# Wider rows for q and causal k, paired P1 blocks, earlier first outputs and later transposes in an attention-plus-MLP kernel

## Chip, cores and metric

One core of a Trainium2 chip. The metric is the device time of one execution in microseconds (us). Times are medians of several executions, with the range in brackets. The profile is one execution of the same program; its span is some 1.8 us shorter than the time of the same execution.

A ratio of two kernels is the mean time of one kernel's runs over that of the other's of the same rounds, so it is not quite the ratio of the medians that are quoted. Its 95% interval stands in brackets behind it.

## The reference

Four batches of eight heads, 768 tokens, head dimension 64. Three heads attend causally ("retrieval"); five see only four sink tokens and a window of 64. The attention output goes through a two-layer MLP with a per-feature leaky slope.

```python
# q, k, v: (4, 8, 768, 64) float32; is_retrieval = [1,0,1,0,0,0,1,0]; n_sink 4, window 64
scores = matmul(q, k.T) / sqrt(64)
mask   = causal                      # retrieval heads
mask   = causal & (sink | in_window) # the other heads
a = softmax(where(mask, scores, -1e9)); attn = matmul(a, v)
x = attn.transpose(0, 2, 1, 3).reshape(3072, 512)
h = x @ w_in                                   # (512, 2048)
out = (max(h, 0) + alpha * min(h, 0)) @ w_out  # (2048, 512)
```

## The kernel before

Work goes in 16 pairs of heads, four to a batch. "P1" is the product with w_in, "P2" the one with w_out. Pairs 0 to 3 run while data and weights load. Then the first P1 block follows, and from pair 4 on P1 and P2 of the last batch fill TensorE between the attention pieces. All of q, k and v are loaded as float32, cast to bfloat16, and transposed on TensorE for pairs 0 to 7. The parts that matter here:

```python
def load_pair(n, src, dst, eng):              # q or k of both heads: ONE transfer, rows of two tokens (512 B)
    flat = dst.rearrange("p a b d -> p (a b d)")[:, 0:12 * D]
    T = rows_of(n)                            # 2 for pairs 0 to 7, 1 after
    eng.dma_start(flat.rearrange("p (x y) -> p x y", y=T * D),
                  dram(src, base, [[T * D, 128], [128 * T * D, 12 // T], [1, T * D]]))

def load_v(n): ...                            # one transfer for each head, and a short one for a windowed head

gate = const.tile([128, 1], fp32, name="gate")
nc.gpsimd.tensor_copy(gate, vf[2][:, 5, 1, D - 1:D])   # weights start only after v of pair 2
load_w_in(0, 512)                                      # GpSimd issues the weights, q4 and v4 follow on SyncE
...
for n in range(4):                            # pairs 0 to 3
    ...
    if n == 3:                                # k of pair 4 is issued by ScalarE, between exponentials of pair 3
        seq.insert(1, lambda: load_k(4, nc.scalar))
...
# pair n, from 4 on: sa, sb are the score pieces of its two heads, nxt the transposes of pair n + 1
seq = sa[:1] + prev + sa[1:3] + tail + sa[3:5] + nxt[:1] + sa[5:] + nxt[1:] + sb[:1]
seq += [lambda: AV(n, 0)] + sb[1:]
```

The softmax here doesn't subtract the row's maximum and nothing guards it: scores larger than these inputs give would overflow.

Of the kernel before, what the change touches and what calls it, by code (L numbers as in the profile page):

```python
# [8 lines left out]
AF = mybir.ActivationFunctionType  # L9
# [5 lines left out]
def kernel(  # L15
# [89 lines left out]
    def heads(n):  # L105
        return PAIRS[n % 4]

    def rows_of(n):
        return 2 if n < CROSS else 1

    def load_pair(n, src, dst, eng):
        flat = dst.rearrange("p a b d -> p (a b d)")[:, 0:12 * D]
        base = (n // 4 * H + heads(n)[0]) * S * D

        T = rows_of(n)
        eng.dma_start(flat.rearrange("p (x y) -> p x y", y=T * D),
                      dram(src, base, [[T * D, 128], [128 * T * D, 12 // T], [1, T * D]]))

    def load_q(n, eng=nc.sync):
        load_pair(n, q, qf[n % NF], eng)  # L120

    def load_k(n, eng=nc.sync):
        if n >= CROSS:
            load_rows(n, k, kf)
        else:
            load_pair(n, k, kf[n % NF], eng)
# [29 lines left out]
    def cast_pair(n, nat, src, *copies):  # L156
        copy = copies[0]
        flat = src.rearrange("p a b d -> p (a b d)")[:, 0:12 * D]
        if n >= CROSS:
            copy(nat.rearrange("p i (h d) -> p h i d", h=2), flat.rearrange("p (h i d) -> p h i d", h=2, d=D))  # L160
            return
        pairs = flat.rearrange("p (h i t d) -> p h i t d", h=2, t=2, d=D)
        for t in range(2):
            copies[t % len(copies)](nat[:, 3 * t:3 * t + 3, :].rearrange("p i (h d) -> p h i d", h=2), pairs[:, :, :, t, :])

    def whole_q(n):
        nat = natq[n] = NAT0[0][n] if n < 4 else NATQ[n % 2]
        copy = nc.gpsimd.tensor_copy if 0 < n < 6 else nc.scalar.copy if 0 < n < CROSS else nc.vector.tensor_copy
        cast_pair(n, nat, qf[n % NF], copy)
        if n >= CROSS:  # L170
            nc.sync.dma_start(qT[n % NK][:, 0:S].rearrange("p (i r) -> p i r", r=128),
                              nat.rearrange("p i c -> p (i c)"), transpose=True)

    def whole_k(n):
        if n < CROSS:
            natk[n] = NAT0[1][n] if n < 4 else NATK1[n % 2]
            one = nc.gpsimd.tensor_copy if 0 < n < 6 else nc.vector.tensor_copy
            cast_pair(n, natk[n], kf[n % NF], one, nc.scalar.copy if n == 0 else one)
            return
# [94 lines left out]
    def Tq(n):  # L274
        tr = T_bank(natq.pop(n), "mm0" if n < 4 else misc_tag())
        T = rows_of(n)
        nc.scalar.copy(qT[n % NK][:, 0:S].rearrange("d (p t) -> d p t", t=T), in_order(tr[:, 0:S], T))

    def Tk(n):
        tr = T_bank(natk.pop(n), "mm1" if n < 4 else misc_tag())  # L280
        T = rows_of(n)
        for hh, h in enumerate(heads(n)):
            rows = slice(64 * hh, 64 * hh + 64)
# [3 lines left out]
            if RETR[h]:  # L287
                cuts = [0, 256 // T, S // T] if n == 0 else [0, S // T]
# [109 lines left out]
    def X(n):  # L398
        nat = xn.pop(n)
        tr = bank_bf(misc_tag())  # L400
        for i in range(NT):
# [9 lines left out]
    BANKS = {"beside P2": ["mm0", "mm1"], "beside attention": ["mm0", "mm1", "mm2", "m2"],  # L411
             "lead": ["mm0", "mm1", "mm2", "m2", "sc0", "sc1"], "tail": ["mm0", "mm1", "sc0", "sc1"]}
# [7 lines left out]
    def P1(t, f, cs=range(4), where="beside P2"):  # L420
        o, w = TOK[t]
        o %= 2 * S
        psg = half_done.pop((t, f)) if (t, f) in half_done else mm_bank(where)
        for c in cs:
            a = PAIRS[c][0] // 2
            nc.tensor.matmul(psg[:, 0:w], w_in_b[:, a, 128 * f:128 * (f + 1)], xT[:, c, o:o + w],  # L426
                             start=(c == 0), stop=(c == 3))
        if cs[-1] < 3:
# [3 lines left out]
        nc.scalar.activation(neg[:, 0:w], psg[:, 0:w], AF.Relu, scale=-1.0)  # L432
        nc.vector.scalar_tensor_tensor(g_buf[t % 2][:, f, 0:w], neg[:, 0:w], oma[:, f:f + 1], psg[:, 0:w],  # L433
                                       op0=ALU.mult, op1=ALU.add)

    po = {}
    n_po = [0]

    def P2(t, s, quarter):
        if quarter == 0:  # L440
            n_po[0] += 1
            tags = ("mm2", "m2", "m0", "m1") if t > 5 else ("mm2", "m2")
            po[t] = bank(tags[n_po[0] % len(tags)])
        for f in range(4 * quarter, 4 * quarter + 4):
            nc.tensor.matmul(po[t], g_buf[t % 2][:, f, 128 * s:128 * (s + 1)], w_out_b[:, f, :],  # L445
                             start=(f == 0), stop=(f == 15))
        if quarter == 3:
            ot = work.tile([128, 512], fp32, tag="ot", name="ot", bufs=3)
            nc.scalar.copy(ot, po.pop(t))  # L449
# [19 lines left out]
    def p1_units(t, fs=range(16), where="beside P2"):  # L469
        return [(TOK[t][1] / 512, lambda f=f: P1(t, f, where=where)) for f in fs]  # L470

    def p2_units(t):
        return [(1, lambda s=s, u=u: P2(t, s, u)) for s in range(TOK[t][1] // 128) for u in range(4)]
# [11 lines left out]
    def seg_pieces(n):  # L485
# [6 lines left out]
        seq += [lambda: AV(n, 0)] + sb[1:]  # L492
        return seq, (2 + len(sa[1:3]) if tail else 0)
# [15 lines left out]
    gate = const.tile([128, 1], fp32, name="gate")  # L509
    nc.gpsimd.tensor_copy(gate, vf[2][:, 5, 1, D - 1:D])  # L510
# [30 lines left out]
    for n in range(4):  # L541
# [5 lines left out]
        else:  # L547
            seq = [sa[0], last[0], sa[1], last[1]] + sb + [last[2]]
# [18 lines left out]
    AV(3, 0)  # L567
# [46 lines left out]
    second = [p2_units(t) for t in range(8)]  # L614
    hidden = [p1_units(t) for t in range(6)]
    hidden[1][:6] = p1_units(1, range(6), where="beside attention")
    plan = [hidden[1][:6] + merge(second[0], hidden[1][6:]) + second[1][:4],
# [58 lines left out]
```

## Time and profile before

| | before |
|---|---|
| median of 4 runs beside the changed kernel | 251.75 us (250.34 to 252.37) |
| profiled span | 249.1 us |
| TensorE busy | 233.9 us, 94% |
| ScalarE busy | 144.7 us, 58% |
| first score matmul, first w_in matmul, pair 4's first score matmul, first w_out matmul | 7.18, 28.01, 42.88, 53.51 us |
| last matmul ends | 245.83 us |

The prediction below shows the lines that find the bound: TensorE is full except in the loading phase and at the end, and its one large hole is a wait of 5.1 us for q of pair 5 that ends at 51.5 us. The columns are start, time, engine, line, operation, count, and in brackets the idle time before it with what ended it; "ACTq" is ScalarE's sequencer. Short names from here on: "q4" is q of pair 4; natq and natm are the bfloat16 copies of q and k; eR and eS are the exponentials of the causal and of the windowed heads; g holds the hidden values of the MLP; Tq(n), Tk(n) and X(n) are the transposes of q, of k and of the attention output of pair n; sa, sb are the score pieces of its two heads, nxt the transposes of pair n + 1.

### The profile page before, as it was taken

The page shows a single profiled execution, that of the slowest core. Times are in us where ns is not written, and L with a number is a line of the kernel's source. Part 1 is how long each engine was busy: PE and PEld are TensorE (multiplying, and loading weights), DVE is VectorE, ACT ScalarE, POOL GpSimd, SP SyncE. Part 2 cuts the span into 40 slices and gives each one's busy share as a digit, 9 for nine tenths or more (in the row PEclk, how much of TensorE's full clock was granted, in tenths as well). Part 3 has the DMA queues.
Part 4 walks back from the last instruction along what each step waited for, and adds up shares of the span by engine and source line. Part 5 has one row for each costly group of instructions (what it writes and reads, how often), then busy time and mean ns, then how long its engine had stood idle before and what let it go on. Part 6 is the DMA issues. An engine that isn't in the chain of part 4 may idle for free.

```text
span 249.1 us, 5404 instructions
## 1 busy us (share of the span) xinstructions
PE 233.9 (94%) x2059; PEld 146.8 (59%) x2059; DVE 166.6 (67%) x399; ACT 144.7 (58%) x289; POOL 49.0 (20%) x104
## 2 busy tenths in 40 slices
PE   7799799479999999999999999999999999999994
PEld 6688545346767655455667645456676544456653
DVE  7788688617698987888678757976556546743320
ACT  5888188527777567666655656566654355543320
POOL 5559820540104210110102110200000000000000
PEclk9999999959999999999999999999999999999999
DMA  6997999999999998999795981311111101012112
GB/s 191 267 241 143 229 202 197 218 251 266 241 235 142 230 236 182 222 175 188 131 230 121 229 132 45 71 37 43 45 42 42 45 0 42 3 42 84 45 45 84
DMA packets 90882, 34.95 MB, mean 140 GB/s; under 512 B 72408, under 2 KB 89064, under 8 KB 90856
## 3 DMA queue, kind: packets, MB, share of 16 engines
q1 hardware_dynamic: 83448, 24.77, 51.3%
q0 software_dynamic: 5664, 8.91, 15.8%
q10 hardware_dynamic: 1744, 0.93, 1.4%
q8 instruction: 16, 0.26, 0.4%
q14 instruction: 10, 0.08, 0.1%
HBM read 27.46 MB, written 6.29 MB: 136 GB/s over the span
## 4 chain that ended last, share of the span: by engine, by line
PE 62%; DMA 13%; SPq 8%; DVE 8%; ACT 3%; POOL 2%; issue 2%; POOLq 0%; DVEq 0%; ACTq 0%
PE P L445 27%; PE P L426 22%; DMA qf<-in_q_dram 10%; SPq L137 4%; DMA kf<-in_k_dram 4%; PE P L389 3%; SPq L139 3%; PE P L335 3%; DVE g L433 3%; PE P L362 2%; PE P L402 2%; ACT neg L432 1%; PE P L463 1%; PE P L267 1%; POOL vb L191 1%
## 5 line engine op out<-in xcount | busy, mean ns | idle before, releaser
L433 DVE SCALAR_TENSOR_TENSOR g<-neg,oma,P 128x512 bf16<-128x512 f32 (+1 forms) x128 | 77.5, 613 | 48.2 <-ACT neg L432 46.4
L426 PE MATMUL P<-xT,w_in_b 128*128 128x512 bf16 (+1 forms) x512 | 101.2, 327 | 1.4 <-DVE g L433 1.3
L445 PE MATMUL P<-w_out_b,g 128*128 128x512 bf16 x368 | 94.8, 382 | 0.0
L432 ACT ACTIVATE neg<-P 128x512 f32<-128x512 f32 (+1 forms) x128 | 62.9, 493 | 53.3 <-PE P L426 50.1
L426 PEld LDWEIGHTS <-w_in_b 128*128 128x128 bf16 x512 | 48.1, 98 | 34.7 <-issue 2.2
L445 PEld LDWEIGHTS <-g 128*128 128x128 bf16 x368 | 34.4, 98 | 27.4 <-issue 0.6
L343 ACT ACTIVATE eR<-P 128x455 bf16<-128x455 f32 (+3 forms) x63 | 37.9, 608 | 11.5 <-PE P L335 9.3
L369 ACT ACTIVATE eS<-P 128x384 bf16<-128x384 f32 (+1 forms) x55 | 27.8, 519 | 8.7 <-PE P L362 8.1
L452 POOL DMA_DIRECT2D out_dram<-ot x18 | 9.8, 543 | 94.3 <-ACT ot L449 74.9
L335 PE MATMUL P<-qT,kT 128*128 128x454 bf16 (+10 forms) x132 | 24.6, 271 | 1.0 <-DVE kT L290 0.5
L449 ACT COPY ot<-P 128x512 f32<-128x512 f32 x23 | 13.5, 586 | 13.9 <-PE P L445 13.8
L373 DVE TENSOR_TENSOR eS<-eS,ms 128x384 bf16<-128x384 bf16 (+1 forms) x47 | 16.8, 362 | 6.2 <-ACT eS L369 6.1
L362 PE MATMUL P<-qT,kT 128*128 128x192 bf16 (+2 forms) x140 | 20.1, 236 | 0.8 <-ACT eR L343 0.6
L395 DVE TENSOR_TENSOR xn<-P,rcp 128x448 bf16<-128x448 f32 x32 | 20.0, 625 | 1.1
L362 PEld LDWEIGHTS <-kT 128*128 128x128 bf16 x140 | 13.2, 98 | 7.2 <-issue 0.3
L335 PEld LDWEIGHTS <-kT 128*128 128x128 bf16 x132 | 11.6, 98 | 9.5 <-issue 0.9
L347 DVE TENSOR_TENSOR eR<-eR,mr 128x128 bf16<-128x128 bf16 (+4 forms) x54 | 11.3, 226 | 6.5 <-ACT eR L343 6.4
L389 PEld LDWEIGHTS <-eS 128*128 128x128 bf16 x260 | 10.5, 97 | 3.0 <-DVE eS L373 0.4
L153 POOL COPY natk<-natk 4x192 f32<-4x192 f32 x10 | 4.3, 442 | 40.3 <-DVE natk L182 40.3
L389 PE MATMUL P<-vb,eS 128*128 128x65 bf16 x260 | 11.8, 193 | 0.5 <-DVE xT L404 0.3
L389 PEld LDWEIGHTS <-eR 128*128 128x128 bf16 x324 | 11.3, 97 | 1.5
L389 PE MATMUL P<-vb,eR 128*128 128x65 bf16 x324 | 11.7, 192 | 0.0
(82 smaller groups left out, 164.6 us busy)
## 6 DMA issues: line engine op xcount, KB each, us to landing
qf<-in_q_dram SPq DMA_DIRECT2D x16, 384.0 KB
vf<-in_v_dram SPq DMA_DIRECT2D x32, 192.0 KB
out_dram<-ot POOLq DMA_DIRECT2D x18, 256.0 KB, 2.9
kf<-in_k_dram SPq DMA_DIRECT2D x16, 192.0 KB
kf<-in_k_dram SPq DMA_DIRECT2D x6, 384.0 KB
w_in_b<-in_moe_w_in_dram POOLq DMA_DIRECT2D x4, 512.0 KB, 8.5
w_out_b<-in_moe_w_out_dram POOLq DMA_DIRECT2D x4, 512.0 KB, 18.5
out_dram<-ot SPq DMA_DIRECT2D x5, 256.0 KB
```

The source lines that it names most:

```text
L335: nc.tensor.matmul(sc[:, x, a - lo:z - lo], kt[:, 128 * j:128 * (j + 1)], qt[:, c:c + z - a], start=True, stop=not masked)
L343: nc.scalar.activation(e[:, lo:hi].rearrange("p (x c) -> p x c", x=len(parts)), sc[:, 0:len(parts), 0:(hi - lo) // len(parts)], AF.Exp, sc ...
L362: nc.tensor.matmul(sc[:, x, o:o + w], kt[:, 128 * j:128 * (j + 1)], qt[:, 124 * j:124 * j + w], start=True, stop=not on_pe)
L369: nc.scalar.activation(slots, sc[:, 0:len(thirds), 0:384].rearrange("p x (s c) -> p x s c", c=192), AF.Exp, scale=scale)
L373: nc.vector.tensor_tensor(slots, slots, factor, op=ALU.mult)
L389: nc.tensor.matmul(pav[:, i, :], e[:, o:o + 128], vv[:, j, hh, 0:D + 1], start=(m == 0), stop=(m == len(terms) - 1))
L395: nc.vector.tensor_tensor(xn[n][:, :, 64 * hh:64 * hh + 64], pav[:, :, 0:D], rcp.to_broadcast([128, NT, D]), op=ALU.mult)
L426: nc.tensor.matmul(psg[:, 0:w], w_in_b[:, a, 128 * f:128 * (f + 1)], xT[:, c, o:o + w], start=(c == 0), stop=(c == 3))
L432: nc.scalar.activation(neg[:, 0:w], psg[:, 0:w], AF.Relu, scale=-1.0)
L433: nc.vector.scalar_tensor_tensor(g_buf[t % 2][:, f, 0:w], neg[:, 0:w], oma[:, f:f + 1], psg[:, 0:w], op0=ALU.mult, op1=ALU.add)
L445: nc.tensor.matmul(po[t], g_buf[t % 2][:, f, 128 * s:128 * (s + 1)], w_out_b[:, f, :], start=(f == 0), stop=(f == 15))
L449: nc.scalar.copy(ot, po.pop(t))
```

## The change

The intent: fewer, larger packets for q and causal k, so that q of pair 5 is in earlier; pair 5's transposes later; first outputs that need only the part of w_out that has come; fewer instructions on ScalarE. The core of the diff (the helpers that only follow from it are cut):

```diff
+    def row_tokens(n, h=None):
+        return 1 if n >= CROSS else 6 if h is None or RETR[h] else 2
     def load_q(n, eng=nc.sync):
-        load_pair(n, q, qf[n % NF], eng)
+        T = row_tokens(n)                     # 6: rows of 1536 B
+        eng.dma_start(..., dram(q, ..., [[T * D, 128], [128 * T * D, 12 // T], [1, T * D]]))
     def load_k(n, eng=nc.sync):
-            load_pair(n, k, kf[n % NF], eng)
+        for hh, h in enumerate(heads(n)):     # one transfer for each head
+            T = row_tokens(n, h)
+            eng.dma_start(..., dram(k, ..., [[T * D, 128], [128 * T * D, 6 // T], [1, T * D]]))
 ...
     def P1(t, f, ...):
+        blocks = range(f, f + 512 // w)       # two blocks where the tile has 256 tokens
+        for i, fb in enumerate(blocks): ...
-        nc.scalar.activation(neg[:, 0:w], psg[:, 0:w], AF.Relu, scale=-1.0)
+        nc.scalar.activation(neg, psg, AF.Relu, scale=-1.0)
 ...
+        if n == 4:
+            seq = sa + sb[:1] + [lambda: AV(n, 0)] + sb[1:] + nxt
 ...
-    gate = const.tile([128, 1], fp32, name="gate")
-    nc.gpsimd.tensor_copy(gate, vf[2][:, 5, 1, D - 1:D])
     load_w_in(0, 512)
 ...
-            seq = [sa[0], last[0], sa[1], last[1]] + sb + [last[2]]
+            seq = [sa[0], last[0], sa[1], last[1]] + sb + [lambda: AV(3, 0), last[2]]
 ...
+    second[0] = p2_units(0, [(s + i, u) for s in (0, 2) for u in range(4) for i in range(2)])
-    plan = [hidden[1][:6] + merge(second[0], hidden[1][6:]) + second[1][:4],
+    plan = [merge(second[0], hidden[1]) + second[1][:4],
```

More of the change, by code (lines that the diff above doesn't have):

```diff
@@ L106, in heads @@
         return PAIRS[n % 4]
-    def rows_of(n):
-        return 2 if n < CROSS else 1
-    def load_pair(n, src, dst, eng):
-        flat = dst.rearrange("p a b d -> p (a b d)")[:, 0:12 * D]
-        base = (n // 4 * H + heads(n)[0]) * S * D
-        T = rows_of(n)
-        eng.dma_start(flat.rearrange("p (x y) -> p x y", y=T * D),
-                      dram(src, base, [[T * D, 128], [128 * T * D, 12 // T], [1, T * D]]))
+    def row_tokens(n, h=None):
+        return 1 if n >= CROSS else 6 if h is None or RETR[h] else 2
     def load_q(n, eng=nc.sync):
-        load_pair(n, q, qf[n % NF], eng)
+        T = row_tokens(n)
+        for_heads = qf[n % NF].rearrange("p a b d -> p (a b d)")[:, 0:12 * D]
+        eng.dma_start(for_heads.rearrange("p (x y) -> p x y", y=T * D),
+                      dram(q, (n // 4 * H + heads(n)[0]) * S * D, [[T * D, 128], [128 * T * D, 12 // T], [1, T * D]]))
     def load_k(n, eng=nc.sync):
@@ L124, in load_k @@
             load_rows(n, k, kf)
-        else:
-            load_pair(n, k, kf[n % NF], eng)
+            return
+        for hh, h in enumerate(heads(n)):
+            T = row_tokens(n, h)
+            dst = kf[n % NF].rearrange("p a b d -> p (a b d)")[:, 6 * D * hh:6 * D * (hh + 1)]
+            eng.dma_start(dst.rearrange("p (x y) -> p x y", y=T * D),
+                          dram(k, (n // 4 * H + h) * S * D, [[T * D, 128], [128 * T * D, 6 // T], [1, T * D]]))
     def load_v(n):
@@ L153, in sinks @@
                 nc.gpsimd.tensor_copy(vh[:, 1:7, :], vh[:, 0:1, :].to_broadcast([NSINK, 6, D // 2]))
-    def cast_pair(n, nat, src, *copies):
-        copy = copies[0]
-        flat = src.rearrange("p a b d -> p (a b d)")[:, 0:12 * D]
-        if n >= CROSS:
-            copy(nat.rearrange("p i (h d) -> p h i d", h=2), flat.rearrange("p (h i d) -> p h i d", h=2, d=D))
-            return
-        pairs = flat.rearrange("p (h i t d) -> p h i t d", h=2, t=2, d=D)
-        for t in range(2):
-            copies[t % len(copies)](nat[:, 3 * t:3 * t + 3, :].rearrange("p i (h d) -> p h i d", h=2), pairs[:, :, :, t, :])
     def whole_q(n):
@@ L168, in whole_q @@
         copy = nc.gpsimd.tensor_copy if 0 < n < 6 else nc.scalar.copy if 0 < n < CROSS else nc.vector.tensor_copy
-        cast_pair(n, nat, qf[n % NF], copy)
+        flat = qf[n % NF].rearrange("p a b d -> p (a b d)")[:, 0:12 * D]
+        copy(nat.rearrange("p i (h d) -> p h i d", h=2), flat.rearrange("p (h i d) -> p h i d", h=2, d=D))
         if n >= CROSS:
@@ L176, in whole_k @@
             natk[n] = NAT0[1][n] if n < 4 else NATK1[n % 2]
-            one = nc.gpsimd.tensor_copy if 0 < n < 6 else nc.vector.tensor_copy
-            cast_pair(n, natk[n], kf[n % NF], one, nc.scalar.copy if n == 0 else one)
+            for hh, h in enumerate(heads(n)):
+                copy = nc.gpsimd.tensor_copy if 0 < n < 6 else nc.scalar.copy if n == hh == 0 else nc.vector.tensor_copy
+                T = row_tokens(n, h)
+                flat = kf[n % NF].rearrange("p a b d -> p (a b d)")[:, 6 * D * hh:6 * D * (hh + 1)]
+                copy(natk[n][:, :, D * hh:D * (hh + 1)].rearrange("p (t i) d -> p t i d", t=T),
+                     flat.rearrange("p (i t d) -> p t i d", t=T, d=D))
             return
@@ L275, in Tq @@
         tr = T_bank(natq.pop(n), "mm0" if n < 4 else misc_tag())
-        T = rows_of(n)
+        T = row_tokens(n)
         nc.scalar.copy(qT[n % NK][:, 0:S].rearrange("d (p t) -> d p t", t=T), in_order(tr[:, 0:S], T))
@@ L280, in Tk @@
         tr = T_bank(natk.pop(n), "mm1" if n < 4 else misc_tag())
-        T = rows_of(n)
         for hh, h in enumerate(heads(n)):
+            T = row_tokens(n, h)
             rows = slice(64 * hh, 64 * hh + 64)
@@ L287, in Tk @@
             if RETR[h]:
-                cuts = [0, 256 // T, S // T] if n == 0 else [0, S // T]
+                cuts = [0, -(-256 // T), S // T] if n == 0 else [0, S // T]
                 for lo, hi in zip(cuts, cuts[1:]):
@@ L408 @@
     n_mm = [0]
-    BANKS = {"beside P2": ["mm0", "mm1"], "beside attention": ["mm0", "mm1", "mm2", "m2"],
-             "lead": ["mm0", "mm1", "mm2", "m2", "sc0", "sc1"], "tail": ["mm0", "mm1", "sc0", "sc1"]}
+    BANKS = {"beside P2": ["mm0", "mm1"], "lead": ["mm0", "mm1", "mm2", "m2", "sc0", "sc1"], "tail": ["mm0", "mm1", "sc0", "sc1"]}
     def mm_bank(where):
@@ L423, in P1 @@
         psg = half_done.pop((t, f)) if (t, f) in half_done else mm_bank(where)
-        for c in cs:
-            a = PAIRS[c][0] // 2
-            nc.tensor.matmul(psg[:, 0:w], w_in_b[:, a, 128 * f:128 * (f + 1)], xT[:, c, o:o + w],
-                             start=(c == 0), stop=(c == 3))
+        blocks = range(f, f + 512 // w)
+        for i, fb in enumerate(blocks):
+            for c in cs:
+                a = PAIRS[c][0] // 2
+                nc.tensor.matmul(psg[:, w * i:w * (i + 1)], w_in_b[:, a, 128 * fb:128 * (fb + 1)], xT[:, c, o:o + w],
+                                 start=(c == 0), stop=(c == 3))
         if cs[-1] < 3:
@@ L431, in P1 @@
         neg = work.tile([128, 512], fp32, tag="neg", name="neg", bufs=3)
-        nc.scalar.activation(neg[:, 0:w], psg[:, 0:w], AF.Relu, scale=-1.0)
-        nc.vector.scalar_tensor_tensor(g_buf[t % 2][:, f, 0:w], neg[:, 0:w], oma[:, f:f + 1], psg[:, 0:w],
-                                       op0=ALU.mult, op1=ALU.add)
+        nc.scalar.activation(neg, psg, AF.Relu, scale=-1.0)
+        for i, fb in enumerate(blocks):
+            c = slice(w * i, w * (i + 1))
+            nc.vector.scalar_tensor_tensor(g_buf[t % 2][:, fb, 0:w], neg[:, c], oma[:, fb:fb + 1], psg[:, c],
+                                           op0=ALU.mult, op1=ALU.add)
     po = {}
@@ L442, in P2 @@
             tags = ("mm2", "m2", "m0", "m1") if t > 5 else ("mm2", "m2")
-            po[t] = bank(tags[n_po[0] % len(tags)])
+            po[t, s] = bank(tags[n_po[0] % len(tags)])
         for f in range(4 * quarter, 4 * quarter + 4):
-            nc.tensor.matmul(po[t], g_buf[t % 2][:, f, 128 * s:128 * (s + 1)], w_out_b[:, f, :],
+            nc.tensor.matmul(po[t, s], g_buf[t % 2][:, f, 128 * s:128 * (s + 1)], w_out_b[:, f, :],
                              start=(f == 0), stop=(f == 15))
@@ L448, in P2 @@
             ot = work.tile([128, 512], fp32, tag="ot", name="ot", bufs=3)
-            nc.scalar.copy(ot, po.pop(t))
+            nc.scalar.copy(ot, po.pop((t, s)))
             r = TOK[t][0] + s * 128
@@ L467, in P2_last, with p1_units, p2_units @@
             (nc.scalar, nc.sync)[half].dma_start(out[r:r + 128, c], ot[:, 0:256])
-    def p1_units(t, fs=range(16), where="beside P2"):
-        return [(TOK[t][1] / 512, lambda f=f: P1(t, f, where=where)) for f in fs]
-    def p2_units(t):
-        return [(1, lambda s=s, u=u: P2(t, s, u)) for s in range(TOK[t][1] // 128) for u in range(4)]
+    def p1_units(t, where="beside P2"):
+        return [(1, lambda f=f: P1(t, f, where=where)) for f in range(0, 16, 512 // TOK[t][1])]
+    def p2_units(t, order=None):
+        order = order or [(s, u) for s in range(TOK[t][1] // 128) for u in range(4)]
+        return [(1, lambda s=s, u=u: P2(t, s, u)) for s, u in order]
     def seg_scores(n):
@@ L566 @@
         load(n)
-    AV(3, 0)
     AV(3, 1)
@@ L614 @@
     second = [p2_units(t) for t in range(8)]
+    second[0] = p2_units(0, [(s + i, u) for s in (0, 2) for u in range(4) for i in range(2)])
     hidden = [p1_units(t) for t in range(6)]
-    hidden[1][:6] = p1_units(1, range(6), where="beside attention")
-    plan = [hidden[1][:6] + merge(second[0], hidden[1][6:]) + second[1][:4],
+    plan = [merge(second[0], hidden[1]) + second[1][:4],
             merge(second[1][4:], hidden[2]) + merge(second[2], hidden[3]) + second[3][:2],
```

## The prediction

> **What bounds the kernel now.** I read the page's slices, then the waits, then the order of time on TensorE, SyncE, ScalarE and the DMA queues between 20 and 65 us. The slices first; one is 6.2 us:
>
> ```profile
> PE   7799799479999999999999999999999999999994
> PEclk9999999959999999999999999999999999999999
> DMA  6997999999999998999795981311111101012112
> ```
>
> TensorE is full except at the start, in slice 8 (from 43.6 us) and at the end; slice 9 runs at half clock. The DMA engines are full from 6 us to about 100 us. So TensorE bounds the time, and its one large hole lies in the loading phase. The waits name it:
>
> ```profile
> POOL natq L164 <- DMA qf<-in_q_dram: 7.2, 2, 5.4
> PE P L267 <- POOL natq L164: 5.1, 1, 5.1
> ```
>
> and TensorE's timeline shows it:
>
> ```profile
> 45.80 0.60 PE L426 MATMUL P<-xT,w_in_b 128*128 128x256 bf16 x4
> 51.53 0.95 PE L267 MATMUL P<-ident,natq 128*128 128x128 bf16 x6 [5.12 <-POOL natq L164]
> 52.27 1.06 PE L426 MATMUL P<-xT,w_in_b 128*128 128x256 bf16 x4
> ```
>
> TensorE stands 5.1 us because the transposes of q of pair 5 sit in the middle of pair 4 and that q lands at 50.9. The same four 256-column matmuls then run at half clock; the windows agree (PEclk is the number before the DMA share):
>
> ```profile
> 45.00:50.00 5.00, 1.40 (x12) 0.84 (x10) 2.75 (x10) 2.27 (x7) 3.53 (x8) 0.94 1.21 219
> 50.00:55.00 5.00, 3.47 (x17) 2.06 (x18) 0.97 (x3) 1.73 (x3) 1.91 (x4) 0.50 1.07 252
> ```
>
> From 51.5 to about 55.5 the work done takes 4 us instead of 2: the hole costs 5.1 + 2.0 = 7.1 us. From 56 us on TensorE issues nearly back to back: 0.86 us for four 512-column matmuls, 0.43 for four of 256.
>
> Why is q so late? SyncE issued it at 34.63. In the DMA view from 35 to 45 us:
>
> ```profile
> q0 software_dynamic: 1555, 1.54, 90.7%
> q1 hardware_dynamic: 1556, 0.43, 30.5%
> ```
>
> q0 carries the weights, q1 q, k and v. They alternate one packet for one packet: 10 us x 16 engines / 1555 = 103 ns for a pair, of which the weight packet has some 84 and the 256-byte packet 19. A queue's progress beside the weights is counted in packets, not bytes. Until 50.9 q1 had to pass q4 (768 packets of 512 B), v4 (about 1584 of 256 B) and q5 (768): 195 per engine.
>
> **What the Trainium skill says.** "DMA: Bandwidth & Descriptors", section "Queues, rings and completion order": each engine goes round its queues at packet granularity. The 1555 against 1556 above agrees. The same page, "Why small descriptors are slow": a fixed cost per packet. Here 512-byte loads alone move about 290 GB/s and 256-byte ones about 215 (rates in slices of the window from 5 to 10 us), thus 28 and 19 ns a packet per engine. The packet records give 47 ns for 1 KB and 87 for 2 KB, so I put a 1536-byte packet at about 70 ns, an estimate between these, against 3 x 28 = 84 for what it replaces. "TensorE: Matmul & The Clock Gate", "The HAM clock gate": about 3.4 us of idleness halves the clock, and about as much work restores it. The trace agrees: after a 5.1 us gap half clock until about 55.5. "PSUM — Partial Sum Buffer", "The four PSUM rules": groups open together in one bank spoil each other. The new P1 finishes its first block before it starts the second, so this costs nothing; no run here shows it.
>
> **The change part by part.**
>
> *Six-token rows.* q of pairs 0 to 7 goes from 48 to 16 packets per engine, a causal k head from 24 to 8. In engine time that is only 16 x (84 - 70) = 0.22 us for a q and 0.11 for a k head. Up to k of pair 3 that saves 3 x 0.22 + 2 x 0.11 = 0.9 us, and the first q perhaps 0.4 us more. So k of pair 3, which GpSimd waited for until 18.78, comes about 1.3 us earlier. Beside the weights the gain is larger, as it is packets that count. The casts of q become one instruction instead of two (on ScalarE 0.93 for the two, about 0.85 for one); nothing on the path.
>
> *The gate removed.* The first w_in load is issued at 20.28 after v of pair 2 (20.09); without the gate it follows the cast of k of pair 3, 0.4 us sooner. Its first packets come about 2.5 us after the issue (the DMA rate is near zero from 21 to 22.7 us), by which time v of pair 3 is in. With the rows, w_in and q4 (released behind it) start 1.3 + 0.4, say 1.8 us earlier.
>
> *Pair 5 at the end of pair 4.* Its transposes move some 8 us of TensorE work later. New landing of q5: q4 16 + v4 99 + q5 16 = 131 rounds instead of 195; 131 x 84 = 11.0, plus own packets 1.1 + 1.9 + 1.1 and k4 1.2, is 16.3 us. The same sum for before gives 22.3, and measured was 25.4 (the slowest engine lags), so x 1.14: 18.6 us from 23.6, about 42 us. k5, 32 rounds on, about 46. Pair 4 starts at 42.2 (0.9 us earlier: 0.4 from the first q, and 0.5 as AV(3,0) fills the 1.0 us idle at 26.4). Its TensorE work is 3.1 us of scores, values and transposes and six units of 0.86, 8.3 us in all. Tq(5) comes at about 50: no wait. The 5.1 us and the half clock are gone.
>
> *First outputs by parts of w_out.* This makes the filling possible. The parts land at 41.3, 44.7, 48.3 and 52.3 us now (last packets of q0), in about the same places afterwards: 1.8 us earlier start against about 1.3 more of q and k passed between. With two token tiles taken part by part, parts 0 and 1 are all that pair 4 needs, part 2 comes at about 52, part 3 at about 56. No wait.
>
> *Two 256-token blocks per bank.* ScalarE loses 32 x (2 x 389 - 597) ns = 5.8 us of its 144.7; VectorE and TensorE keep theirs. After 56 us TensorE waits only 1.3 us in all on P1's banks, mostly for 512-token blocks. Worth 0 to 0.3 us.
>
> *What takes over.* Total DMA work is nearly conserved, so the next load is hardly earlier: q of pair 6. ScalarE casts it ahead of the first exponential of pair 5:
>
> ```profile
> 59.77 0.93 ACT L164 CAST natq<-qf 128x384 bf16<-128x384 f32 x2
> 60.58 1.25 ACT L343 ACTIVATE eR<-P 128x454 bf16<-128x454 f32 x2
> ```
>
> Before, q6 landed at about 56.4 (v5 was cast at 55.29, then 48 packets of 28 ns). After: 1.8 earlier by the start, 0.9 by cheaper packets (q4, q5, q6, half of k4 and k5), so 53.7. The cast then ends at 54.6 and the first exponential at 55.2. TensorE reaches pair 5 at 50.5, gets through two score pieces, a value product and two units by about 51.7, and stands until 55.2, as both score banks are full. The third score piece of pair 5 started at 61.94 before: 61.94 - 55.2 = **6.7 us gained**. Of the 8.5 us otherwise within reach (7.1 and the earlier start) some 2 are lost to this new wait. The loads of pair 8 have about 6 us of slack (landed by about 69.5, v cast at 75.3), so they follow. The rest shifts unchanged: 251.7 - 6.7 = 245.0.
>
> **The rivals.** (1) *The new 3.5 us stand trips the clock too.* It is at the edge of the 3.4 us window; half clock would cost 1.7 to 2 us: gain about 4.8, 246.9 us. I give it a third. (2) *The stall moves whole:* as the DMA bytes are conserved, q6 comes no earlier than before, for instance if the earlier w_in does not materialise. The profile speaks for conservation (DMA full from 25 to 60), against it that DMA stands almost still from 21 to 22.7. The gain is then 61.94 - 57.9 = 4.0, 247.7 us; a fifth. (3) *Nothing takes over:* SyncE, whose issues took up to 9 us for v5, runs ahead with fewer packets and q6 comes by 51; all 8.5 us: 243.2. One tenth. (4) *w_in or w_out late:* larger q4 packets delay w_in's last part (landed 37.9, used at about 38.8). It starts 1.8 earlier, so at most 0.5 us is lost.
>
> **Range and chances.** Mixing 245.0 with rivals 1 to 3 gives about 245.7. The range runs from rival 3 to somewhat beyond rival 2, 243.2 to 248.6. The border of 2% is 246.7; rivals 1 and 2 are beyond it, but not all of their mass, so faster 0.65, same 0.33, slower 0.02.
>
> **What would show it.** Right, if the wait of Tq for natq of 5.1 us is gone; w_in is issued near 18.5; the first P2 matmul lies near 43 instead of 53.5; a wait of ScalarE for q of pair 6 appears at 51 to 55 with a TensorE gap of 2 to 4 us; ScalarE's busy time falls by about 6 us, TensorE's matmuls stay. Wrong, if q5 still lands after 48, if TensorE waits for w_out, or if time is gained or lost after 70 us.

## More of the kernel before

One more view matters afterwards: ScalarE's order of time around the load that it issues itself.

```profile
23.13 0.81 ACT L369 ACTIVATE eS<-P 128x768 bf16<-128x768 f32 x1 [0.26 <-PE P L362]
23.21 0.39 ACTq L116 DMA_DIRECT2D kf<-in_k_dram  x1
24.11 0.49 ACT L369 ACTIVATE eS<-P 128x384 bf16<-128x384 f32 x1 [0.17 <-PE P L362]
```

The issue of k of pair 4 takes the sequencer 0.39 us, beside a running exponential. It costs nothing.

## The result, and the profile after

The changed kernel takes 259.13 us (258.36 to 260.18, 4 runs) against 251.75: ratio 1.030 [1.025, 1.036]. It is slower, and outside the predicted range.

| | before | after |
|---|---|---|
| median | 251.75 us | 259.13 us |
| profiled span | 249.1 | 256.6 |
| TensorE busy, matmuls | 233.9, 2059 | 233.5, 2059 |
| first score matmul | 7.18 | 8.09 |
| first w_in matmul | 28.01 | 39.49 |
| pair 4's first score matmul | 42.88 | 54.55 |
| first w_out matmul | 53.51 | 56.72 |
| last matmul ends | 245.83 | 253.31 |

The slices of the page after (6.4 us each) beside those in the prediction:

```profile
PE   7699039979899999999999999999999899999994
PEclk9999858999999999999999999999999999999999
DMA  7999999999923999999394891131101101011212
```

TensorE has the same work. The hole that was in slice 8 is gone, but slices 5 and 6 (25.7 to 38.5 us) hold a larger one, and it has its own half clock. The windows give its size (span of time, then busy time and count of PE, weight loads, VectorE, ScalarE and GpSimd, then clock, DMA share and GB/s):

```profile
25.00:30.00 5.00, 0.98 (x19) 0.83 (x16) 1.18 (x3) 0.00 (x0) 3.12 (x5) 0.96 1.13 238
30.00:35.00 5.00, 0.00 (x0) 0.00 (x0) 0.00 (x0) 0.00 (x0) 1.27 (x2) 0.50 1.22 197
35.00:40.00 5.00, 3.45 (x41) 3.00 (x41) 2.63 (x8) 1.68 (x3) 0.00 (x0) 0.51 1.20 215
```

From 30 to 35 us TensorE, VectorE and ScalarE all do nothing. The waits say who holds whom (engine, tile, line, what ended the wait, total, times, longest):

```profile
ACT eS L365 <- DMA vf<-in_v_dram: 11.0, 1, 11.0
...
PE P L358 <- ACT eS L365: 10.6, 2, 10.4
```

TensorE waits for an exponential on ScalarE (the score banks are full), and ScalarE waits for a load of **v**. No exponential reads v. So look at what ScalarE's sequencer does there:

```profile
24.04 0.81 ACT L365 ACTIVATE eS<-P 128x768 bf16<-128x768 f32 x1 [0.26 <-PE P L358]
24.06 11.64 ACTq L125 DMA_DIRECT2D kf<-in_k_dram  x2
35.80 1.19 ACT L365 ACTIVATE eS<-P 128x384 bf16<-128x384 f32 x2 [10.95 <-DMA vf<-in_v_dram]
```

The same place that took 0.39 us before now holds two issues and takes 11.64. The chain of work shows what lies between the two (start, time, what):

```profile
23.38 11.84 DMA vf<-in_v_dram
...
35.24 0.04 ACTq L125
...
35.31 0.39 ACTq L125
...
35.80 0.50 ACT eS L365
...
36.34 0.32 PE P L358
```

ScalarE's second issue starts only after v of pair 4, issued by SyncE at 23.38, has landed. The program as compiled names the wait. (A semaphore is a counter on which one instruction waits until another has raised it.) Each ordinary transfer of SyncE and ScalarE is given one of eight completion semaphores, DMAHW0 to DMAHW7, in turn; a transfer carries a wait for the previous transfer with the same semaphore. (In the lists of before and after, this holds for each of their 134 and 142 transfers but the first eight.) Building the kernels gives the list of instructions with their waits; the traces do not name semaphores. Shortened, on ScalarE before and after, and the transfer of v on SyncE after (a wait can stand on a semaphore instruction just ahead of the transfer):

```
before  ACT  DMACopy kf <- in_k  128x6x128   [waits DMAHW4, DVE]
after   ACT  DMACopy kf <- in_k  128x384     [waits DMAHW1]
after   ACT  DMACopy kf <- in_k  128x3x128   [waits DMAHW3, DMAHW2, DVE]
after   SP   DMACopy vf <- in_v  128x6x64    [waits DMAHW3]      (v of pair 4, first head)
```

Reckoned in the order of allocation, the turn goes q4 on semaphore 2, v4 on 3, 4 and 5, q5 on 6, k5 on 7 and 0, k4's first half on 1, one transfer of v5 on 2, k4's second half on 3. That is the semaphore of v4's first head, and v4 travels beside the weights: 11.84 us. The single k4 of before had semaphore 4, last used by v of pair 3, which had landed by then.

One thing the prediction did foretell is there as well: with the q rows there is no wait for natq any more. Two new waits of TensorE come with the rest of the change:

```profile
PE P L445 <- DVE g L433: 1.8, 1, 1.8
...
PE P L331 <- ACT kT L286: 0.9, 1, 0.9
```

The sums agree roughly: pair 4 starts 11.7 us later (54.55 against 42.88), the end is 7.5 us later (253.31 against 245.83). Of the difference, 4.2 us, the vanished hole gave back 7.1 and the two new waits took 2.7: 4.4. (By windows of the kernel before, 56.00 to 56.20 us is still at 0.50 and 56.20 to 56.50 at 0.98. So the half clock lasted to 56.2 and not to 55.5, the hole cost nearer 5.1 + 4.7 / 2 = 7.5 us, and the sum is 4.8.)

### The profile page after: what moved, and what is told of

Its sections match the earlier page's. It is cut to its first block, busy times and chain, and to the rows that moved or that the text cites. A ratio compares the mean times of both kernels' runs of the same rounds, so it can differ in the third digit from the quotient of the medians.

```text
span 256.6 us, 5348 instructions
## 1 busy us (share of the span) xinstructions
PE 233.5 (91%) x2059; PEld 147.2 (57%) x2059; DVE 163.9 (64%) x398; ACT 142.8 (56%) x255; POOL 47.9 (19%) x98
## 4 chain that ended last, share of the span: by engine, by line
PE 77%; DMA 8%; DVE 5%; ACT 5%; issue 1%; POOL 1%; ACTq 0%; SPq 0%; DVEq 0%; POOLq 0%
PE P L445 30%; PE P L424 29%; DMA vf<-in_v_dram 7%; PE P L385 6%; PE P L331 4%; PE P L358 3%; DVE g L433 3%; PE P L398 2%; ACT neg L430 2%; DMA qf<-in_q_dram 2%; PE P L463 1%; ACT eR L339 1%; PE P L263 1%; DVE xn L391 1%; POOL vb L187 1%
## 5 line engine op out<-in xcount | busy, mean ns | idle before, releaser
L433 DVE SCALAR_TENSOR_TENSOR g<-neg,oma,P 128x512 bf16<-128x512 f32 (+1 forms) x128 | 74.8, 612 | 49.3 <-ACT neg L430 47.7
L424 PE MATMUL P<-xT,w_in_b 128*128 128x512 bf16 (+1 forms) x512 | 95.7, 326 | 1.4 <-DVE g L433 1.4
L445 PE MATMUL P<-w_out_b,g 128*128 128x512 bf16 x368 | 92.1, 379 | 1.8 <-DVE g L433 1.8
L430 ACT ACTIVATE neg<-P 128x512 f32<-128x512 f32 x96 | 57.1, 598 | 60.3 <-PE P L424 55.2
L339 ACT ACTIVATE eR<-P 128x455 bf16<-128x455 f32 (+3 forms) x63 | 37.6, 604 | 13.6 <-PE P L331 10.6
L365 ACT ACTIVATE eS<-P 128x384 bf16<-128x384 f32 (+1 forms) x55 | 27.8, 519 | 21.5 <-DMA vf<-in_v_dram 11.0
L385 PEld LDWEIGHTS <-eS 128*128 128x128 bf16 x260 | 11.3, 100 | 4.1 <-DVE eS L369 0.8
L385 PE MATMUL P<-vb,eS 128*128 128x65 bf16 x260 | 12.5, 198 | 0.9 <-DVE eS L369 0.6
L153 POOL COPY vb<-vb 4x192 f32<-4x192 f32 x20 | 7.0, 363 | 26.1 <-DVE vb L187 24.9
```

Of the source, the lines that this page charges most:

```text
L339: nc.scalar.activation(e[:, lo:hi].rearrange("p (x c) -> p x c", x=len(parts)), sc[:, 0:len(parts), 0:(hi - lo) // len(parts)], AF.Exp, sc ...
L365: nc.scalar.activation(slots, sc[:, 0:len(thirds), 0:384].rearrange("p x (s c) -> p x s c", c=192), AF.Exp, scale=scale)
L385: nc.tensor.matmul(pav[:, i, :], e[:, o:o + 128], vv[:, j, hh, 0:D + 1], start=(m == 0), stop=(m == len(terms) - 1))
L424: nc.tensor.matmul(psg[:, w * i:w * (i + 1)], w_in_b[:, a, 128 * fb:128 * (fb + 1)], xT[:, c, o:o + w], start=(c == 0), stop=(c == 3))
L430: nc.scalar.activation(neg, psg, AF.Relu, scale=-1.0)
L433: nc.vector.scalar_tensor_tensor(g_buf[t % 2][:, fb, 0:w], neg[:, c], oma[:, fb:fb + 1], psg[:, c], op0=ALU.mult, op1=ALU.add)
```

## The experiments

Theory A: the wait of ScalarE's second k transfer for its completion semaphore stops ScalarE and, through full score banks, TensorE. Rival B: the other parts are to blame (order of P1 and P2, pair 5 late, no gate). Rival C: the second transfer waits for its queue or for room beside the weights. Fifteen kernels ran, all with correct results; e1 to e8 ran on one chip, e9 to e15 on another. Runs of the kernel before went beside each batch, and those of earlier batches on the same chip are counted in: medians of 251.23 us for e1 to e4, 251.72 for e5 to e8, 251.14 for e9 to e12, 251.16 for e13 to e15.

### Is it the split of k? (e1, e2, e3)

**e1**: the changed kernel, k of pair 4 alone in one transfer.

```diff
+        if n == 4:    # one transfer for both heads, two-token rows; Tk and whole_k take T = 2 for it
+            eng.dma_start(kf..., dram(k, ..., [[2 * D, 128], [256 * D, 6], [1, 2 * D]])); return
```

> The changed kernel with k of pair 4 alone loaded by one transfer (two-token rows) instead of two. Theory A (the second of the two transfers on ScalarE's queue reuses the completion semaphore of v of pair 4, which is still in flight, and holds up the exponentials behind it from 24 to 35 us): the 11 us wait of ScalarE and the 10.4 us gap of TensorE at 26 us vanish, pair 4 starts near 43.5 us instead of 54.6, time about 248.5 us, 246 to 251. Theory B (the wider rows and the earlier weights slow the loads themselves, and the order on ScalarE does not matter): still above 256 us with a gap of 8 us or more before 40 us.

Measured: 247.15 us (247.09 to 248.34), ratio 0.983 [0.977, 0.989]; 12 us less than the changed kernel. ScalarE's order of time:

```profile
23.97 0.81 ACT L369 ACTIVATE eS<-P 128x768 bf16<-128x768 f32 x1 [0.26 <-PE P L362]
24.07 0.42 ACTq L123 DMA_DIRECT2D kf<-in_k_dram  x1
24.95 0.49 ACT L369 ACTIVATE eS<-P 128x384 bf16<-128x384 f32 x1 [0.17 <-PE P L362]
```

The stand is gone, and with it the whole loss. B is out for the loss. The bytes are the same.

**e2**: the changed kernel, both transfers of k4 issued by SyncE.

```diff
-            seq.insert(1, lambda: load_k(4, nc.scalar))
+            seq.insert(1, lambda: load_k(4))
```

> The changed kernel with both transfers of k of pair 4 issued by SyncE instead of ScalarE. Theory A: no wait of ScalarE near 24 us, as nothing stands before its exponentials; but k of pair 4 now lies behind v of pair 4, lands near 40 to 43 us and may hold Tk(4) up by 0 to 2 us: about 249.5 us, 247 to 252. Theory B: above 256 us as before.

Measured: 250.68 us (249.67 to 253.14), ratio 0.997 [0.989, 1.005]. ScalarE goes through its exponentials, but k4 comes late. GpSimd waits 11.0 us for it in one piece, of which TensorE passes on 0.7:

```profile
POOL natm L173 <- DMA kf<-in_k_dram: 14.5, 3, 11.0
...
PE P L263 <- POOL natm L173: 0.7, 1, 0.7
```

Off the engine that has the exponentials, the split costs far less. Why e2 is still 3.5 us above e1 is not settled: in the profiled execution 2.2 us of it were there before the weights were used at all (first w_in matmul 30.59 against 28.40; the clock was at half from 8.4 to 11.8 us), and that is not the late k4.

**e3**: the kernel before with nothing but each k load split into two transfers.

```diff
-            load_pair(n, k, kf[n % NF], eng)
+            for hh in range(2):   # one head each, two-token rows as before
+                eng.dma_start(..., dram(k, ..., [[2 * D, 128], [256 * D, 3], [1, 2 * D]]))
```

> The kernel before with nothing changed but that k of each pair up to 7 is loaded by two transfers of one head each, in two-token rows as before. Theory A: the same wait of ScalarE appears, from about 23.5 us until the first head of v of pair 4 lands at 38 to 40 us; part of it is given back as q of pair 5 no longer comes late: 257 to 263 us. Theory B (wide rows or early weights at fault): within 1% of before, 250 to 254 us.

Measured: 261.30 us (258.68 to 261.71), ratio 1.038 [1.031, 1.046]. ScalarE waits for the same load:

```profile
ACT eS L372 <- DMA vf<-in_v_dram: 12.2, 1, 12.2
```

The split alone, without a single changed row, reproduces the loss in the kernel before. So the split is enough to cause it, and e1 shows that without it at pair 4 it is gone.

### Is it the semaphore's turn? (e9)

**e9**: the changed kernel with k of pair **5** in one transfer, k of pair 4 still in two on ScalarE. One transfer fewer ahead moves k4's second half onto the semaphore of q of pair 4, which comes in sooner than v4. The compiled program says so: its wait is DMAHW2 in place of DMAHW3.

```diff
+        if n == 5:    # as in e1, but for pair 5
```

> The changed kernel with k of pair 5 (not of pair 4) in one transfer. Pair 4's k stays in two transfers on ScalarE's stream; but one transfer fewer ahead of it in the rotation moves its second half onto the completion semaphore that q of pair 4 used last, instead of v of pair 4. That q was in by 30.1 us in the changed kernel, v's first head at 35.2. If the stand of ScalarE is the wait for the semaphore of the transfer eight places earlier: ScalarE's exponential of pair 3 waits until about 30.2, some 5.5 us instead of 10.95, on q of pair 4; time about 253 (251 to 255). Rival: the second transfer waits on ScalarE's own queue (its first half not landed) or for room beside the weights, whatever the rotation says: the stand stays 10 to 12 us and the time 258 to 260. Second rival: TensorE's loss is mainly the half clock after the gap, which a 5 us gap trips too: then the time is nearer 255.

Measured: 252.03 us (251.92 to 252.82), ratio 1.003 [0.998, 1.007]. ScalarE, then TensorE:

```profile
26.09 4.17 ACTq L129 DMA_DIRECT2D kf<-in_k_dram  x2
30.37 1.64 ACT L369 ACTIVATE eS<-P 128x384 bf16<-128x384 f32 x3 [3.49 <-DMA qf<-in_q_dram]
```

```profile
30.91 0.24 PE L362 MATMUL P<-qT,kT 128*128 128x192 bf16 x1 [2.90 <-ACT eS L369]
```

and the chain of work:

```profile
22.95 6.86 DMA qf<-in_q_dram
...
29.83 0.02 ACTq L129
...
29.88 0.39 ACTq L129
```

Nothing about k4's own transfers was touched, yet the stand now ends with q4 and is 3.49 us instead of 10.95. That rules out C: with a full queue or no room beside the weights, the form of k5 could not have done this. In this run k of pair 5 is issued at 31.30, after the stand has ended, so it cannot have acted by its own traffic: the turn is fixed when the program is compiled, and a transfer that is issued later can still be counted ahead. (C was a fair rival: in the changed kernel SyncE took 4.28 us to issue the short tail of v4 at 24.62, though the last user of its semaphore, a part of v of pair 2, had been in since 19.2. What holds such issues no run shows.) The stand is shorter than my 5.5 us because this execution was 2.0 us later when it reached that point (26.09 against 24.06; its clock was at half from 9.4 to 12.8 us); its end, 29.83, is near the 30.2 where I put it.

### Which part brings the gain? (e7, e8, e6, e4, e5)

**e7**: the kernel before with q in six-token rows and nothing else; k stays one transfer.

```diff
-        load_pair(n, q, qf[n % NF], eng)
+        load_pair(n, q, qf[n % NF], eng, 6 if n < CROSS else 1)   # the casts and Tq follow
```

> The kernel before with q in six-token rows and nothing else (k and v as before, gate kept, no other order). If progress beside the weights is counted in packets, q of pair 5 lands at 45 to 47 us instead of 50.9, the 5.1 us hole shrinks to under 1 us and the clock stays full: 245.5 to 248.5 us. If bytes count, q lands at about 50.5 us and the time stays at 251 to 252.

Measured: 246.03 us (245.63 to 248.60), ratio 0.980 [0.972, 0.987]. The 5.1 us hole is gone: GpSimd casts q of pair 5 at 45.53 without a wait for it, where it had waited until 50.97. The bytes are the same, so progress beside the weights went by packets, as the prediction had it. What is left in that stage is a wait for k of pair 5:

```profile
50.37 0.79 PE L268 MATMUL P<-ident,natm 128*128 128x128 bf16 x6 [1.55 <-POOL natm L164]
```

**e8**: the kernel before with only pair 5's transposes at the end of pair 4.

```diff
+        if n == 4:
+            seq = sa + sb[:1] + [lambda: AV(n, 0)] + sb[1:] + nxt
```

> The kernel before with pair 5's transposes at the end of pair 4 and nothing else. The hole of 5.1 us at 46 us is gone, but q of pair 5 (50.9 us), its k (53.6 us) and q of pair 6 (56.4 us) come as before, so TensorE waits 3 to 4 us in all between 49 and 58 us instead: 248 to 250 us. If the move alone were the cure: under 246 us.

Measured: 249.64 us (247.63 to 250.79), ratio 0.990 [0.981, 0.999]. TensorE still waits for the old q rows, but less:

```profile
53.80 0.79 PE L267 MATMUL P<-ident,natq 128*128 128x128 bf16 x6 [2.25 <-POOL natq L164]
```

**e6**: e1 with pair 5's transposes back in the middle of pair 4.

```diff
-        if n == 4:
-            seq = sa + sb[:1] + [lambda: AV(n, 0)] + sb[1:] + nxt
```

> The run with k of pair 4 in one transfer, with pair 5's transposes put back into the middle of pair 4 (undoes that part alone). q of pair 5 was cast at 44.9 us there, so if the wider rows alone remove the hole, nothing is lost: 246 to 248 us, and the 0.9 us wait of the first scores of pair 5 for kT vanishes. If the move is what removes it, a wait of TensorE of 3 us or more returns and the time is 250 us or more.

Measured: 247.94 us (247.78 to 248.15), ratio 0.985 [0.979, 0.991]. No wait for natq returned, and the wait for kT of 0.9 us went away. The median is 0.8 us above e1's; the profiled execution made its first score matmul 0.9 us later than e1's (8.93 against 8.02) and was at half clock from 8.7 to 12.1 us, so I read no loss from it. Together the three say: the rows of q remove the hole by themselves; the late transposes half remove it without them and are not needed with them.

**e4**: the changed kernel with every k of pairs 0 to 7 in one transfer of two-token rows.

```diff
+        if n < CROSS:    # as in e1, for all pairs that TensorE transposes
```

> The changed kernel with k of every pair up to 7 loaded by one transfer in two-token rows; q stays in six-token rows and all other parts stay. Theory A: no wait of ScalarE, and the first scores no longer start 0.9 us late (8.1 against 7.2 us), which was the second transfer of k of pair 0: about 247.5 us, 245 to 250. Theory B: above 255 us, as q's wide rows and the missing gate are still there.

Measured: 247.69 us (247.36 to 247.88), ratio 0.984 [0.978, 0.990]. The first score matmul is at 7.41 instead of 8.09. The wait that I had predicted to take over appears:

```profile
55.94 0.83 ACT L164 CAST natq<-qf 128x768 bf16<-128x768 f32 x1 [1.66 <-DMA qf<-in_q_dram]
```

It is 1.66 us on ScalarE where I had 3.5, and TensorE passes on only 0.25 us of it (a wait for eR at 57.27).

**e5**: k of pairs 0 and 4 in one transfer, and one P1 unit ahead of the first P2 in pair 4.

```diff
-    plan = [merge(second[0], hidden[1]) + second[1][:4],
+    plan = [hidden[1][:1] + merge(second[0], hidden[1][1:]) + second[1][:4],
```

> The changed kernel with k of pairs 0 and 4 each by one transfer, and a P1 unit instead of a P2 unit as the first unit of pair 4. If the 0.9 us late first scores come from the split of k of pair 0, and the 1.8 us wait of the first P2 matmul at 45.4 us (in the run with k of pair 4 in one transfer) from its bank being the last one of the leading P1, both vanish: 2 to 2.5 us under that run, so about 245 us. The rival, that the loads set the pace of pair 5 anyway (q of pair 6), leaves the time at 246.5 to 247.5 us, with a wait of ScalarE for q of pair 6 of 1 to 3 us.

Measured: 247.14 us (246.69 to 247.15), ratio 0.981 [0.974, 0.988]. My 245 was missed and the rival held: the wait ahead of the first P2 matmul fell from 1.82 to 0.53, but the time stayed. In the waits:

```profile
ACT natq L164 <- DMA qf<-in_q_dram: 1.2, 1, 1.2
...
PE P L449 <- DVE g L437: 0.5, 1, 0.5
```

TensorE waits 1.03 us for kT and 0.76 for xn in the same stage. With one wait out of the way the next ones appear.

### The two blocks, the gate, and a best version (e10 to e15)

**e10**: e7 with two 256-token P1 blocks per bank.

```diff
+        blocks = range(f, f + 512 // w)          # P1, its activation and its VectorE step as in the change
```

> The kernel before with q in six-token rows (246.0) and, beside it, two 256-token P1 blocks per bank: that part of the change by itself. My prediction put it at 0 to 0.3 us of gain. From the milestones of the earlier runs (pair 4 to pair 7 takes 27.8 us with one block per bank and 28.5 to 29.2 with two) I now rather expect a loss: 246.6 (245.5 to 247.5). ScalarE's busy time falls by 5 to 6 us. Rival: the shorter ScalarE work pays, 245.3 to 245.8.

Measured: 249.14 us (247.18 to 250.72), ratio 0.990 [0.985, 0.995]: 3 us above e7 (on the other chip). But this run also had TensorE's wait for k of pair 5 at 2.17 us instead of 1.55, and a half clock behind it, which e7 hadn't (its clock is 1.00 throughout):

```profile
52.00:54.00 2.00, 2.00 (x31) 1.72 (x30) 1.49 (x4) 0.48 (x2) 0.26 (x1) 0.50 1.15 317
```

So it could not be read as the price of two blocks.

**e11**: e7 without the gate. **e12**: e11 with only the k transposes of pair 5 later.

```diff
-    gate = const.tile([128, 1], fp32, name="gate")                 # e11, e12
-    nc.gpsimd.tensor_copy(gate, vf[2][:, 5, 1, D - 1:D])
+        if n == 4:                                                  # e12
+            seq = sa[:5] + nxt[:1] + sa[5:] + sb[:1] + [lambda: AV(n, 0)] + nxt[1:] + sb[1:]
+            return seq, 0
```

> The kernel before with q in six-token rows (246.0) and the gate ahead of the first w_in load removed. w_in is issued 0.4 to 1 us sooner; q and k of pair 5 come that much sooner or stay. Expected 245.5 (244.8 to 246.3), Tk(5)'s wait for k of pair 5 (1.55) shrinking to 0.5 to 1.2. Rival: the weights' packets now go beside v of pair 3 and q, k, v get no earlier, so nothing changes, 245.8 to 246.5, or k of pair 5 later and 247.

> As the last, and only the k transposes of pair 5 a little later in pair 4 (after its first value product), as the 1.55 us wait of Tk(5) for k of pair 5 is the last hole left in that stage. Expected: this wait gone, 244.3 (243.5 to 245.5). Rival: the copy of kT then ends too late for pair 5's first score piece and a wait of 0.5 to 0.9 for kT takes its place, 245 to 246.

Measured: e11 247.57 us (245.21 to 248.36), ratio 0.983 [0.978, 0.988]; e12 245.89 us (245.29 to 246.90), ratio 0.978 [0.974, 0.982]. Taking the gate away gained nothing that shows. In e12 the wait for k of pair 5 falls to 0.59 us, but one of 1.18 for q of pair 5 stands ahead of it; my 244.3 was missed.

**e13**: e1 with one 256-token block per bank. **e14**: e12 with two. **e15**: e12 with the gate.

```diff
-        for i, fb in enumerate(blocks): ...     # e13: P1 as in the kernel before
+        blocks = range(f, f + 512 // w)         # e14: P1 as in the change
+    gate = const.tile([128, 1], fp32, name="gate")   # e15
```

> The changed kernel with k of pair 4 in one transfer (247.15) and one 256-token P1 block per bank as before. If the two blocks per bank cost time: 245.5 (244.5 to 246.3), and pair 4 to pair 7 (from X(4) to X(7)) back at about 27.8 us from 28.5. Rival, the cost lies in the order of the first output tiles (their wait for a P2 bank of 1.8 us) or in nothing real: 246.7 to 248.

> The kernel of q rows, no gate and later k transposes of pair 5 (245.9) with two 256-token P1 blocks per bank. There is no wait over 1.2 us in pair 4, so no half clock. If two blocks cost by themselves (coarser pieces between the attention, VectorE later for xn): 247 (246.5 to 248), X(4) to X(7) at 28.5 to 29. Rival: what they cost in the earlier run was the longer wait and its half clock: 245.5 to 246.3.

> The kernel before with q in six-token rows and the k transposes of pair 5 a little later, gate kept. The wait of 1.55 us for k of pair 5 falls to 0.6 or less: 245.2 (244.5 to 246.2). Rival: the gate's removal did help in the run without it: 246.0 to 246.6, no better than q rows alone.

Measured: e13 248.52 us (246.83 to 248.65), ratio 0.986 [0.982, 0.990]; e14 247.80 us (246.64 to 248.17), ratio 0.984 [0.981, 0.988]; e15 246.08 us (245.14 to 247.01), ratio 0.979 [0.975, 0.982].

Taking the two blocks out of e1 did not help (on the other chip), so nothing says that they are why e1 stays above e7. In e14 the medians are 1.9 us above e12, with ranges that overlap; in the two traces the fourth pair of the second batch is reached at the same time (the transposes of its output, 85.8 against 85.7) and the last matmul ends 0.45 us later (241.60 against 241.15). I had read a loss from the longer time between pair 4 and pair 7 (29.0 against 27.8); but pair 4 was reached 1.1 us sooner (56.8 against 57.9), so that is work moved across the mark, not added. But that trace is of the fastest of e14's executions (246.64 us); the means of the six, on one chip, are 247.53 and 246.02. And e10's two executions at full clock took 247.2 and 247.9 us against 245.6 to 246.1 for the three of e7. So beside the q rows a loss of about 1.5 us is likelier than none, while e13 against e1 shows none. What two blocks cost or bring is somewhere between nothing and 2 us of loss, and stays open.

e7, e12 and e15 lie within 0.2 us of one another in the median. They beat both kernels, and what they share is the rows of q. The gain over the kernel before is clear of noise; whether it reaches 2% is not (the intervals span 0.98).

## Why the prediction was wrong

**The step that failed** is "Pair 4 starts at 42.2 (0.9 us earlier ...)", and behind it the way in which the rows were priced. I counted k's packets and its bytes, and took the change of k for one of packet size. It also makes two transfers of one, and I did not ask where the second one stands: in the middle of ScalarE's exponentials. Pair 4's scores started at 54.55. The waits of TensorE and ScalarE of the kernel before could not show it, as the one transfer there waits for nothing; the diff and the untouched line `load_k(4, nc.scalar)` together could. No rival of mine had it: all four were about which data comes late, none about an issue that holds up the compute of its engine.

The other steps, as far as the runs show them:

- *The rows take q of pair 5's wait away*: right, shown by e7. I put its landing at 42 and no run shows it exactly; in e1 GpSimd takes it up at 44.90 without a wait. k of pair 5, put at 46, came at 47.68 in e1 and 49.81 in e7.
- *w_in earlier*: issued at 17.85 instead of near 18.5 (20.21 before). No run shows a gain from it: without the gate e11 was not faster than e7.
- *First q perhaps 0.4 us earlier*: wrong in sign. With k of pair 0 split, the first score matmul went from 7.18 to 8.09. With k in one transfer it is at 7.41 (e4) and 7.38 (e5), and with the q rows alone at 7.18 (e7), so the rows brought nothing there; the start differs by up to a microsecond between executions, so the size is loose.
- *First outputs by parts: "No wait"*: wrong by 1.8 us, and the thing waited for was not w_out. The first P2 comes straight behind the last P1 of its tile and waits for VectorE to write g. Likewise kT is now copied just ahead of pair 5, another 0.9.
- *q of pair 6 takes over with 3.5 us*: too large. It came when I said, roughly (54.4 in e5, 55.9 in e4, against 53.7). But TensorE reached pair 5 at 54.94 in e1, not at 50.5: pair 4 started at 43.28 and had the 2.7 us of new waits in it. So in e1 ScalarE did not wait for that q at all.
- *The gain of 6.7 us*: without the stall, e1 gains 251.23 - 247.15 = 4.1. The hole of 7.1 us, less 2.7 of new waits and 0.4 of later start, is 4.0 (4.4 with the hole at 7.5). The mechanism, a hole traded for smaller waits, was right; the waits were others than mine.
- *ScalarE's busy time falls by about 6 us*: the instructions did, the busy time didn't. The P1 steps' durations add up to 62.9 us before and 57.1 after, 5.8 less, to the tenth what I had worked out; the engine's busy time went from 144.7 to 142.8. The groups of ScalarE add up to more than its busy time, so neighbours overlap at their ends, by 13.6 us in all before and 9.2 after: the short ones must have overlapped more. The groups before and after (line, engine, operation, tiles, shapes, count, then busy us and mean ns):

```profile
L432 ACT ACTIVATE neg<-P 128x512 f32<-128x512 f32 x64 | 38.0, 597 | 31.8 <-PE P L426 30.0 <-DVE xn L395 1.1
L432 ACT ACTIVATE neg<-P 128x256 f32<-128x256 f32 x64 | 24.9, 389 | 21.5 <-PE P L426 20.1 <-DVE xn L395 1.3
```

```profile
L430 ACT ACTIVATE neg<-P 128x512 f32<-128x512 f32 x96 | 57.1, 598 | 60.3 <-PE P L424 55.2 <-issue 1.4 <-DVE eS L369 1.3
```

Slips of the prediction that change nothing: v4 is 768 + 768 + 24 = 1560 packets, not 1584; 0.9 us before 42.88 is 42.0, not 42.2; 7.1 and 0.9 are 8.0, not 8.5; the mix with the chances as stated gives 246.0, not 245.7; the DMA line stays at 7 or more until about 130 us, not 100.

**On the Trainium skill.** "DMA: Bandwidth & Descriptors", "Rules for kernel authors", says of spreading DMAs over SP, ACT and GpSimd that "it only saves sequencer issue time". For bandwidth no run contradicts it. But the issuing engine mattered for another reason: the same two transfers make 259.13 us of total time from ScalarE and 250.68 from SyncE (e2). The same page, "Why a DMA increments its semaphore by 16 and not by 1", wants one semaphore for each transfer in flight; the wait that bit here is how a set of eight keeps to that. Of the four places in the prediction, the clock gate fits again: after 10.36 us of idleness TensorE was granted 0.51 from 35 to 40.

## What to carry to other kernels

Count transfers, not only bytes and packets: where an ordinary transfer takes one of a few completion semaphores in turn, each transfer also waits for the one that had it before, on the sequencer of the engine that issues it. Issue loads from an engine whose compute is on the path only if their semaphore's last user is sure to have landed, and look for untouched call sites whose callee now issues more. When a wait in a trace names a tile that the instruction does not read, look at what the sequencer stands at.

## What the Trainium skill lacked or had wrong

- "DMA: Bandwidth & Descriptors", "Rules for kernel authors": issuing from another engine "only saves sequencer issue time". The row lacks that an issue which must wait stops that engine's compute; the page says only, under "Anatomy of one DMA", that such a wait happens on the issuing sequencer. It cost 10.95 us of ScalarE here for a second transfer of k, 0.39 us for one that had nothing to wait for. In e9 the stand was 3.49 us.
- No page that I found says that a program may give its transfers eight completion semaphores in turn, so that how many transfers come ahead decides what a transfer waits for. Joining an unrelated load (k of pair 5) moved the wait from v to q of pair 4 and the time from 259.13 to 252.03 us.
- "TensorE: Matmul & The Clock Gate", "The HAM clock gate", gives about 3.4 us of idleness for the halving, in a window that runs freely. The window's length fits: the traces' clock records show half clock for 3.41 us (e10), 6.83 (before) and 10.24 (after). The idleness needed does not: a gap of 2.17 us (e10, 48.30 to 50.47) was followed by 0.50 from 52 to 54 us, while one of 2.90 us (e9) left the clock at 1.00. In e10 TensorE stood for only 1.9 of the 3.41 us before the halving at 51.96. That e9 escaped may be because its gap lay across two windows, which no run tests.
